# Seven block products for four in the first layer of a feed-forward block, with the second layer's split weights kept in device memory

## The chip, the cores and the metric

The kernel runs on one core of a Trainium2 chip. The metric is the device time of one execution in microseconds. The core has a matrix engine (TensorE, PE in the profile), three engines for elementwise work (VectorE or DVE, ScalarE or ACT, GpSimd or POOL), and SyncE (SP), which issues the transfers here. Each engine works through its instructions in order; semaphores order them against each other. Matmul results are accumulated in PSUM, eight banks of 128 x 512 float32; everything else lies in SBUF, 128 partitions wide.

## What is computed

An attention with keys and values pooled by eight along the sequence, then a two-layer feed-forward network with a squared ReLU. The inputs are float32 but for the two weights, which are float64.

```python
# batch 8, heads 8, sequence 576, head size 64
k_p = k.reshape(B, H, S // 8, 8, D).mean(axis=3)
v_p = v.reshape(B, H, S // 8, 8, D).mean(axis=3)
attn = softmax(q @ k_p.transpose(0, 1, 3, 2) / sqrt(D))
x = (attn @ v_p).transpose(0, 2, 1, 3).reshape(4608, 512)
h = np.maximum(x @ w_in, 0.0)          # w_in 512 x 2048
out = h * h @ w_out                    # w_out 2048 x 512
```

## The kernel before

The 4608 tokens are worked in 12 chunks of 384 (`NCH`, `CH`), the 2048 hidden columns in 16 blocks of 128 (`NFC`). One *step* is one chunk c and one block fc, so there are 192 steps. In a step TensorE does `hidden(c, fc)` (line 500), which forms h transposed, 128 hidden columns by 384 tokens, and `project(c, fc)` (line 537) of the step two before (`LAG`), which multiplies three token tiles of 128 by the 512 columns of w_out. The sums of `project` stay in three PSUM banks for a whole chunk and are stored at its end.

Chunk 0 multiplies in plain float32, which the trace lists as two matmuls for each product. From chunk 1 on every operand is split: a high half rounded to float32r (an ACT copy) and a low half, the difference (DVE); `split` on line 126 does both. A product is then three matmuls: high by high, high by low, low by high. A step of `hidden` has 4 contraction blocks x 3 = 12 matmuls of 384 columns, a step of `project` 3 tiles x 3 = 9 matmuls of 512 columns. Each matmul has a weight load of its own, 128 columns wide in these two.

The weights come as float64 words. `land` loads a tile of 512 KB, `magnitude` (two ACT operations) and `to_float32` (three DVE operations) turn it into float32, and `split_weights` (line 176) splits it; all of them share 33 slots of 4 KB a partition (`w_tile`, line 134). The 32 split tiles stay in SBUF to the end. A tile of w_in holds two blocks of 128 rows and 256 columns.

The work of a step is written out by hand from line 676: `hidden`, then TensorE's part of the attention for later chunks, then `project`, then on ACT and DVE the split of the previous step's h (`split_hidden`), what the attention stages ask for, the conversions of weights, the loads, and at the end `activate`, which takes this step's h out of PSUM (relu on ACT, the square on DVE from chunk 2 on). `at(step, f, ...)` puts a piece of other work at a step. The attention of a chunk is spread over the 22 steps before it: `STEADY` on line 86 gives for each pair of heads the step of `transpose_q`, `scores`, `exponents`, the sums' way through device memory and back, and `weigh_values` (line 470), which leaves x of that pair split in `xh` and `xl`. Two PSUM banks (`ps_h`) take turns for h.

Before step 0 the attention of chunk 0 runs alone. `FIRST` (line 82) says how many tiles of w_in are converted before it ends: their ACT part stands in the loop at line 618, and lines 585 to 588 load `FIRST + 2` weight tiles ahead of the values of batch 1 (`load_v_pair(1, p)`).

Of the kernel before, what the change touches and what calls it, by code (L numbers as in the profile page):

```python
# [37 lines left out]
def pooled_attn_relu2_ffn(  # L38
# [16 lines left out]
    PE, DVE, ACT, GP, SP = (InOrder(tc, e) for e in (nc.tensor, nc.vector, nc.scalar, nc.gpsimd, nc.sync))  # L55
# [29 lines left out]

# [6 lines left out]
    WC = 256  # L92
# [3 lines left out]
    sb = ctx.enter_context(tc.tile_pool(name="sb", bufs=2))  # L96
    dram = ctx.enter_context(tc.tile_pool(name="dram", bufs=3, space=bass.MemoryType.DRAM))
    ps_o = ctx.enter_context(tc.tile_pool(name="ps_o", bufs=1, space=bass.MemoryType.PSUM))
    ps_h = ctx.enter_context(tc.tile_pool(name="ps_h", bufs=2, space=bass.MemoryType.PSUM))
# [18 lines left out]
    def load(dst, src):  # L118
        loads.append((dst, src))
# [12 lines left out]
    raw, wf, wt = {}, {}, {}  # L132

    def w_tile(dt, name):
        return wts.tile([P, 2, 512], dt, name=name, tag="w", bufs=2 * NFC + 1)

    halves = {}

    def half_tile(kind, name):

        if kind not in halves:
            halves[kind] = w_tile(F32, name)
            return halves[kind][:, 0, :]
        return halves.pop(kind)[:, 1, :]

    def land(key):
        t = raw[key] = w_tile(U32, "raw_" + "_".join(map(str, key)))
        if key[0] == "i":
            _, cb, c0 = key
            load(t, w_in[c0 * P:(c0 + 2) * P, cb * 2 * WC:(cb + 1) * 2 * WC].rearrange("(c p) n -> p c n", p=P))  # L150
        else:
            load(t.rearrange("p a n -> p (a n)"), w_out[key[1] * P:(key[1] + 1) * P, :])

# [2 lines left out]
    def magnitude(key):  # L156

        words = raw[key].rearrange("p a (n w) -> p a n w", w=2)
        wf[key] = half_tile("f", "wf_" + "_".join(map(str, key)))
# [16 lines left out]
    def split_weights(key, eng):  # L176
        t = wt[key] = w_tile(F32R, "w_" + "_".join(map(str, key)))
        split(t[:, 0, :], t[:, 1, :], wf[key], eng)

    kv, kf, loaded = {}, {}, {}  # L180

# [271 lines left out]
    def token_turn(c, p):  # L453
# [13 lines left out]

        return then

    def weigh_values(c, p):  # L470

        if p == 0 and c == 0:
            xts[c] = sb.tile([P, NPAIR, CH], F32, name=f"x_{c}", tag="xh", bufs=2)
        elif p == 0:
            xts[c] = (sb.tile([P, NPAIR, CH], F32R, name=f"xh_{c}", tag="xh", bufs=2),
                      sb.tile([P, NPAIR, CH], F32R, name=f"xl_{c}", tag="xl", bufs=2))
        sc, rb = live.pop((c, p))
        av = ps_a.tile([P, 512], F32, name=f"av_{c}_{p}", tag="a")
        for b, o, n in segments(c):
            for i in range(2):  # L480
                PE.matmul(av[i * D:(i + 1) * D, o:o + n], lhsT=kv[b][2][:, 2 * p + i, :], rhs=sc[:, i, o:o + n],
                                 start=True, stop=True)

        def then():
            if c == 0:
                ACT.copy(xts[c][:, p, :], av[:, :CH])
                return
            xh, xl = xts[c]
            if c == 1:
                split(xh[:, p, :], xl[:, p, :], av[:, :CH])  # L490
                return
            DVE.tensor_tensor(rb, av[:, :CH], rb, op=ALU.mult)
            split(xh[:, p, :], xl[:, p, :], rb)

        return then

    gts = {}


    def hidden(c, fc):  # L500
        hp = ps_h.tile([P, 512], F32, name=f"h_{c}_{fc}", tag="h")
        cb, o = fc * P // WC, fc * P % WC
        prods = []
        for cc in range(NCC):
            key, cols = ("i", cb, cc // 2 * 2), slice(cc % 2 * WC + o, cc % 2 * WC + o + P)
            if c == 0:
                prods += [(wf[key][:, cols], xts[c][:, cc, :])]
            else:
                prods += [(wt[key][:, w, cols], xts[c][x][:, cc, :]) for w, x in ((0, 0), (0, 1), (1, 0))]
        for i, (w, x) in enumerate(prods):  # L510
            PE.matmul(hp[:, :CH], lhsT=w, rhs=x, start=i == 0, stop=i == len(prods) - 1)

        def activate():
            if c == 0:
                r = sb.tile([P, CH], F32, name=f"r_{c}_{fc}", tag="gh", bufs=LAG + 1)
            else:
                r = sb.tile([P, CH], F32, name=f"r_{c}_{fc}", tag="r", bufs=2)
            ACT.activation(r, hp[:, :CH], AF.Relu)
            if c < 2:
                ACT.activation(r, r, AF.Square)  # L520
            else:
                DVE.tensor_tensor(r, r, r, op=ALU.mult)
            gts[c, fc] = r

        return activate
# [36 lines left out]
    def at(step, f, *a):  # L562
        work.setdefault(max(step, -PRO), []).append((f, a))
# [13 lines left out]

    need = {}
    for fc in range(NFC):
        for c0 in range(0, NCC, 2):  # L580
            need.setdefault(("i", fc * P // WC, c0), fc)
        need["o", fc] = fc + LAG
    keys = sorted(need, key=need.get)
    first_keys = keys[:FIRST]
# [74 lines left out]
    for c in range(1, NCH):  # L659
        first, offsets = EARLY if c == 1 else STEADY  # L660
        names = (transpose_q, token_scores, token_normalise, token_turn, weigh_values) if c == 1 else stages
        for b, _, _ in segments(c):
            if b not in ready:
                ready.add(b)
                kv_steps(b, c * NFC + KV0)
        for p in range(NPAIR):
            s = c * NFC + first[p]
            if c > 1 or p:
                at(s - QL, load_q, c, p)
            for d, f in zip(offsets, names):  # L670
                at(s + d, f, c, p)


    last = (to_float32, split_weights)
    on_pe = (transpose_k, transpose_q, scores, token_scores, token_turn, weigh_values, pool_v_pair)
    for s in range(-PRO, len(steps) + LAG):
        todo = work.get(s, [])
        activate = hidden(*steps[s]) if 0 <= s < len(steps) else None
        later = [f(*a) for f, a in sorted(((f, a) for f, a in todo if f in on_pe), key=lambda x: x[0] is weigh_values)]
        store = project(*steps[s - LAG]) if s >= LAG else None  # L680
        if 0 <= s - 1 < len(steps):
            split_hidden(*steps[s - 1])
        for f in later:
            f()
        for f, a in todo:
            if f not in on_pe + last:
                f(*a)
        keys = [a[0] for f, a in todo if f is to_float32]
        if keys:
            to_float32(*keys)  # L690
        for f, a in todo:
            if f is split_weights:
# [35 lines left out]
```

## Time and profile before

| what | us |
|---|---|
| median of 2 runs | 971.47 (971.05 to 971.9) |
| the profiled execution | 972.07 |
| its span, first to last instruction | 970.4 |
| first matmul of `hidden` starts at | 52.59 |
| chunk 0 to the start of chunk 1 | 95.7 |
| chunk 2 to the start of chunk 3 | 76.3 |
| chunk 11 to the end of its last step's `hidden` | about 67 |

The profile page gives for each engine its busy time and the number of instructions; PEld is the weight loads, which run beside the matmuls. Matmuls overlap and their ends are modelled, so the recorded length of one (337 ns for 384 columns) is more than the time that it adds; that is read from the starts. All instructions carry line 34, the helper that issues them, and are told apart by the tiles that they write and read: `h<-xh,w_i` is a matmul that writes h from xh and a tile of w_in. A tile's name in the trace is that of the slot's kind, so `wf_o` can stand for a tile of w_in that reuses the place. The chain of waits follows the last instruction back to what released it.

### The profile page before, as it was taken

The numbers are of one execution on the slowest core, as the hardware profiler recorded it, in microseconds if no ns is written. First come the engines' busy times: TensorE is split into PE (matmuls) and PEld (weight loads), VectorE is DVE, ScalarE is ACT, GpSimd is POOL, SyncE is SP. The second block draws the span as 40 slices with busy tenths as digits, with TensorE's granted clock in tenths as the row PEclk, the third lists the DMA queues.
The fourth block names the chain that finished last, engine by engine and source line by source line (L and its number), as shares of the span: only waits on it lengthen the run. The fifth ranks groups of instructions, "written<-read, shape, count | busy, mean of one in ns | idle before, by whom it ended". The sixth has DMA issues, their size and how long they took to land.

```text
span 970.4 us, 13371 instructions
## 1 busy us (share of the span) xinstructions
PE 947.7 (98%) x4788; PEld 789.8 (81%) x4788; DVE 601.3 (62%) x1066; ACT 431.2 (44%) x911; POOL 330.7 (34%) x191
## 2 busy tenths in 40 slices
PE   7799999999999999999999999999999999999998
PEld 6455557888888888888888888888888888888997
DVE  7466778777676656667766656667677564453221
ACT  2387767675334334334434434443434433432322
POOL 4100034354344444434344344433434434440000
PEclk9589999999999999999999999999999999999999
DMA  9955002113112112112211202222311210200000
GB/s 272 336 191 158 23 7 76 43 43 101 45 45 75 32 34 73 42 41 90 60 38 48 73 17 50 66 46 54 92 41 41 76 32 18 58 9 9 33 1 32
DMA packets 105762, 63.64 MB, mean 66 GB/s; under 512 B 77840, under 2 KB 86880, under 8 KB 105696
## 3 DMA queue, kind: packets, MB, share of 16 engines
q1 hardware_dynamic: 105696, 62.79, 23.3%
q8 instruction: 37, 0.61, 0.3%
q14 instruction: 29, 0.24, 0.1%
HBM read 53.08 MB, written 9.68 MB: 65 GB/s over the span
## 4 chain that ended last, share of the span: by engine, by line
PE 89%; DMA 4%; DVE 3%; SPq 2%; ACT 1%; issue 1%; DVEq 0%; ACTq 0%
PE o L34 40%; PE h L34 40%; PE av L34 4%; PE sps L34 3%; SPq L34 2%; DMA vv<-in_v_dram 2%; DMA k<-in_k_dram 1%; PE vps L34 1%; DVE vp L34 1%; PE pps L34 1%; DMA rc<-rs 1%; DVE kp L34 0%; DVE gl L34 0%; PE kps L34 0%; DVE st L34 0%
## 5 line engine op out<-in xcount | busy, mean ns | idle before, releaser
L34 PE MATMUL h<-xh,w_i 128*128 128x384 f32 x1408 | 391.2, 338 | 0.0
L34 PE MATMUL o<-w_o,gh 128*128 128x512 f32 x1056 | 335.0, 398 | 0.0
L34 POOL PARTITION_ALL_REDUCE tot<-sc x80 | 201.5, 2566 | 223.8 <-issue 214.3
L34 PEld LDWEIGHTS h<-xh,w_i 128*128 128x128 f32 x1408 | 258.0, 188 | 8.3 <-ACT r L34 0.5
L34 PE MATMUL h<-xl,w_i 128*128 128x384 f32 x704 | 236.4, 336 | 0.0
L34 PEld LDWEIGHTS o<-w_o,gh 128*128 128x128 f32 x1056 | 192.6, 189 | 51.7 <-issue 16.5
L34 POOL PARTITION_ALL_REDUCE mx<-sc x80 | 116.5, 1504 | 301.1 <-ACT sc L34 295.0
L34 PE MATMUL o<-w_o,gl 128*128 128x512 f32 x528 | 208.8, 395 | 0.0
L34 DVE TENSOR_TENSOR r<-r 128x384 f32<-128x384 f32 x160 | 105.4, 659 | 144.6 <-ACT r L34 144.6
L34 DVE TENSOR_TENSOR gl<-r,gh 128x384 fp32r<-128x384 f32 x176 | 107.4, 610 | 79.9 <-ACT gh L34 78.3
L34 ACT ACTIVATE r<-h 128x384 f32<-128x384 f32 x192 | 94.0, 490 | 111.3 <-PE h L34 111.3
L34 ACT CAST gh<-r 128x384 fp32r<-128x384 f32 x176 | 90.4, 514 | 117.5 <-DVE r L34 116.1
L34 PEld LDWEIGHTS h<-xl,w_i 128*128 128x128 f32 x704 | 132.2, 188 | 8.2 <-issue 0.7
L34 PEld LDWEIGHTS o<-w_o,gl 128*128 128x128 f32 x528 | 99.1, 188 | 22.2
L34 DVE TENSOR_TENSOR st<-qs,st 64x384 fp32r<-64x384 f32 x80 | 70.3, 879 | 30.2 <-ACT st L34 28.9
L34 ACT CAST st<-qs 64x384 fp32r<-64x384 f32 x80 | 40.9, 511 | 47.0 <-DVE qs L34 46.0
L34 ACT ACTIVATE sc<-sc 72x384 f32<-72x384 f32 x80 | 39.7, 525 | 44.9 <-DVE sc L34 44.9
L34 ACT CAST xh<-rb 128x384 fp32r<-128x384 f32 x40 | 20.5, 513 | 81.1 <-DVE rb L34 81.1
L34 ACT COPY sc<-sps 72x384 f32<-72x384 f32 x80 | 34.1, 475 | 49.5 <-PE sps L34 49.5
L34 DVE TENSOR_REDUCE vp<-v 72x64 f32<-72x512 f32 x48 | 50.9, 1060 | 0.0
L34 PE MATMUL av<-sc,vp 72*64 72x384 f32 (+1 forms) x256 | 46.4, 448 | 2.7 <-ACT sc L34 2.7
L34 DVE TENSOR_REDUCE kp<-k 96x64 f32<-96x512 f32 x42 | 43.5, 1035 | 0.1
(93 smaller groups left out, 739.9 us busy)
## 6 DMA issues: line engine op xcount, KB each, us to landing
k<-in_k_dram SPq DMA_DIRECT2D x48, 192.0 KB
out_dram<-ob SPq DMA_DIRECT2D x36, 256.0 KB
raw_i<-in_moe_w_in_dram SPq DMA_DIRECT2D x16, 512.0 KB
raw_o<-in_moe_w_out_dram SPq DMA_DIRECT2D x16, 512.0 KB
rb<-rd SPq DMA_DIRECT2D x80, 96.0 KB
v<-in_v_dram SPq DMA_DIRECT2D x48, 144.0 KB
q<-in_q_dram SPq DMA_DIRECT2D x112, 48.0 KB
vv<-in_v_dram SPq DMA_DIRECT2D x8, 288.0 KB
```

Source lines behind the costliest of these rows:

```text
L34: return lambda *a, **k: self.tc.keep_in_program_order(f(*a, **k))
```

## The change

From chunk 2 on (`PLAIN = 2`) two steps together compute a 2 x 2 block product: two hidden blocks by two halves of the contraction on the side of the weights, two halves of the contraction by two halves of the tokens (192 each, `HT`) on the side of x. Instead of eight block products it makes seven, from sums of blocks of the weights (S1 to S4) and of x (T1 to T4). Each block product is 2 contraction blocks x 3 split terms, six matmuls of 192 columns. Four products stand in the even step, three in the odd one; between them ACT and DVE add results to each other in the PSUM banks X and Y, and later matmuls accumulate onto these sums.

- `seven` takes the place of `plain` (the old `hidden`). The two h of a pair are taken out of PSUM together at the end of the odd step, and their squares move from DVE to ACT. `split_hidden` moves from the step after to just before `project`, two steps after.
- x of a chunk is kept in float32 (`xf`), and `x_operand` forms and splits seven operands of it at the steps -9 to 0 of the chunk.
- A tile of w_in now holds 128 rows of four blocks. `split_quarter` splits its four quarters a group; `sum_of_quarters` forms and splits S1 to S4 on top. The slots are 32.
- w_out's split tiles don't stay: `store_weights` writes each to device memory at steps 10 to 25, and `fetch_weights` reads it back for each chunk from 1 on, three steps before its `project`.
- `FIRST` is 4.

```diff
+    PLAIN = 2
-    FIRST, EAGER, AHEAD = 2, 8, 5
+    FIRST, EAGER, AHEAD = 4, 8, 5
...
+    GB = 4
+    HT = CH // 2
+    SLOTS, XB, STREAM = 32, 8, 3
...
+    def split_quarter(g, e, kh):
+        split_operand(g, f"A{e}{kh}", quarter(g, e, kh))
...
+    def sum_of_quarters(g, name):
+        a, b, op = {"S1": ((1, 0), (1, 1), ALU.add), "S2": ("S1", (0, 0), ALU.subtract),
+                    "S3": ((0, 0), (1, 0), ALU.subtract), "S4": ((0, 1), "S2", ALU.subtract)}[name]
+        a, b = (sums[x] if isinstance(x, str) else quarter(g, *x) for x in (a, b))
+        t = sums[name] = in_blocks(half_tile("S", f"s_{g}_{name}"))
+        DVE.tensor_tensor(t, a, b, op=op)
+        split_operand(g, name, t)
...
+    def store_weights(fc):
+        t = w_tile(F32R, f"w_o_{fc}")
+        split(t[:, 0, :], t[:, 1, :], wf.pop(("o", fc)))
+        stored[fc] = kept.tile([P, 2, 512], F32, name=f"kept_{fc}")
+        dma(stored[fc], t.bitcast(F32))
+
+    def fetch_weights(c, fc):
+        t = wt["o", fc] = w_tile(F32R, f"w_o_{c}_{fc}")
+        load(t.bitcast(F32), stored[fc])
...
+    def x_operand(c, name):
+        one, two = xf[c][:, :2, :].rearrange("p c (h t) -> p h c t", h=2), xf[c][:, 2:, :].rearrange("p c (h t) -> p h c t", h=2)
+        if name == "T1":
+            src = temps["T"] = sb.tile([P, 2, HT], F32, name=f"t_{c}", tag="t", bufs=1)
+            DVE.tensor_tensor(src, one[:, 1], one[:, 0], op=ALU.subtract)
+        elif name == "T2":
+            src = temps["T"]
+            DVE.tensor_tensor(src, two[:, 1], src, op=ALU.subtract)
...
+        x = xts[c, name] = x_tile(F32R, f"x_{c}_{name}")
+        hi, lo = (x[:, w, :].rearrange("p (c t) -> p c t", c=2) for w in range(2))
+        split(hi, lo, src)
...
+    def seven(c, fc):
+        g, r = fc // GB, fc % GB // 2
+        if fc % 2 == 0:
+            pair["X"], pair["Y"] = (ps_h.tile([P, 512], F32, name=f"h_{c}_{fc + i}", tag="h") for i in range(2))
+        X, Y = pair["X"], pair["Y"]
+        a, b, u, d = X[:, :HT], X[:, HT:CH], Y[:, :HT], Y[:, HT:CH]
+        def product(out, wn, xn, clear=False, end=False):
+            n = 0
+            for k in range(2):
+                cols = slice((k * 2 + r) * P, (k * 2 + r + 1) * P)
+                for i, j in three:
+                    PE.matmul(out, lhsT=wt[g, wn][:, i, cols], rhs=xts[c, xn][:, j, k * HT:(k + 1) * HT],
+                              start=clear and n == 0, stop=end and n == 5, skip_group_check=True)
+                    n += 1
+        if fc % 2 == 0:
+            product(a, "A00", "B11", True)
+            product(b, "S2", "T2")
+            product(u, "S3", "T3", True)
+            product(d, "S1", "T1")
...
+            def soon():
+                ACT.copy(first, a)
+                DVE.tensor_tensor(second, b, first, op=ALU.add)
+                DVE.tensor_tensor(u, u, second, op=ALU.add)
+                DVE.tensor_tensor(b, d, second, op=ALU.add)
+            def at_end():
+                ACT.copy(third, u)
+                DVE.tensor_tensor(d, d, third, op=ALU.add)
+            return soon, at_end
+        product(b, "S4", "B22")
+        product(a, "A01", "B21", end=True)
+        product(u, "A11", "T4", end=True)
+        return [(fc - 1, X), (fc, Y)]
...
-        at(14 + int(i * 0.48), split_weights, key, DVE)
+    for i in range(NFC):
+        at(12 + i, split_quarter, i // GB, i % GB // 2, i % 2)
+        at(10 + i, store_weights, i)
+        at(4 * (5 + i // 4) + i % 4, sum_of_quarters, i // 4, f"S{i % 4 + 1}")
+        for c in range(1, NCH):
+            at(c * NFC + i + LAG - STREAM, fetch_weights, c, i)
...
+        if c >= PLAIN:
+            for d, name in ((-9, "B11"), (-2, "T1"), (-2, "T2"), (-1, "T3"), (-1, "B22"), (0, "B21"), (0, "T4")):
+                at(c * NFC + d, x_operand, c, name)
...
+        for t in (s - 2, s - 1):
+            if 0 <= t < len(steps) and (steps[t][0] < PLAIN) == (t == s - 1):
+                split_hidden(*steps[t])
         store = project(*steps[s - LAG]) if s >= LAG else None
-        if 0 <= s - 1 < len(steps):
-            split_hidden(*steps[s - 1])
+        if soon:
+            soon()
         for f in later:
             f()
...
         issue_loads()
-        for f in (activate, store):
-            if f:
-                f()
+        if activate:
+            activate()
+        for f, a in todo:
+            if f is x_operand:
+                f(*a)
+        if store:
+            store()
```

More of the change, by code (lines that the diff above doesn't have):

```diff
@@ L91, in pooled_attn_relu2_ffn @@
     NKT = H * SP_ // QT
-    WC = 256
+    GB = 4
+    HT = CH // 2
+    SLOTS, XB, STREAM = 32, 8, 3
     const = ctx.enter_context(tc.tile_pool(name="const", bufs=1))
@@ L134, in w_tile @@
     def w_tile(dt, name):
-        return wts.tile([P, 2, 512], dt, name=name, tag="w", bufs=2 * NFC + 1)
+        return wts.tile([P, 2, 512], dt, name=name, tag="w", bufs=SLOTS)
     halves = {}
@@ L148, in land @@
         if key[0] == "i":
-            _, cb, c0 = key
-            load(t, w_in[c0 * P:(c0 + 2) * P, cb * 2 * WC:(cb + 1) * 2 * WC].rearrange("(c p) n -> p c n", p=P))
+            _, g, c = key
+            load(t.rearrange("p a n -> p (a n)"), w_in[c * P:(c + 1) * P, g * 2 * GB * P:(g + 1) * 2 * GB * P])
         else:
@@ L174, in to_float32, with in_blocks, quarter, split_operand @@
             DVE.scalar_tensor_tensor(m, words[..., 1], 0x80000000, m, op0=ALU.bitwise_and, op1=ALU.bitwise_or)
-    def split_weights(key, eng):
-        t = wt[key] = w_tile(F32R, "w_" + "_".join(map(str, key)))
-        split(t[:, 0, :], t[:, 1, :], wf[key], eng)
+    def in_blocks(t):
+        return t.rearrange("p (c r n) -> p c r n", c=2, r=GB // 2)
+    def quarter(g, e, kh):
+        return wf["i", g, "both", kh].rearrange("p c (r e n) -> p e c r n", r=GB // 2, e=2)[:, e]
+    def split_operand(g, name, src):
+        t = wt[g, name] = w_tile(F32R, f"w_{g}_{name}")
+        split(in_blocks(t[:, 0, :]), in_blocks(t[:, 1, :]), src)
+    def split_quarter(g, e, kh):
+        split_operand(g, f"A{e}{kh}", quarter(g, e, kh))
+    sums = {}
+    def sum_of_quarters(g, name):
[5 more added lines that the diff above has]
+        split_operand(g, name, t)
+    stored = {}
+    def store_weights(fc):
[6 more added lines that the diff above has]
+        load(t.bitcast(F32), stored[fc])
     kv, kf, loaded = {}, {}, {}
@@ L468, in token_turn, with x_tile @@
         return then
+    def x_tile(dt, name):
+        return sb.tile([P, 2, CH], dt, name=name, tag="x", bufs=XB)
+    xf = {}
     def weigh_values(c, p):
[L472 to L476, printed above, removed]
+        if c >= PLAIN and p == 0:
+            xf[c] = sb.tile([P, NPAIR, CH], F32, name=f"xf_{c}", tag="xf", bufs=1)
         sc, rb = live.pop((c, p))
@@ L485, in then @@
             if c == 0:
[L486 to L493, printed above, removed]
-        return then
+                x = xts[c, p] = x_tile(F32, f"x_{c}_{p}")
+                ACT.copy(x[:, 0, :], av[:, :CH])
+            elif c < PLAIN:
+                x = xts[c, p] = x_tile(F32R, f"x_{c}_{p}")
+                split(x[:, 0, :], x[:, 1, :], av[:, :CH])
+            else:
+                DVE.tensor_tensor(xf[c][:, p, :], av[:, :CH], rb, op=ALU.mult)
@@ new lines, in weigh_values @@
+        return then
+    temps = {}
+    def x_operand(c, name):
[6 more added lines that the diff above has]
+            DVE.tensor_tensor(src, two[:, 1], src, op=ALU.subtract)
+        elif name == "T4":
+            src = temps["T"]
+            DVE.tensor_tensor(src, two[:, 0], src, op=ALU.subtract)
+        elif name == "T3":
+            src = one[:, 1]
+            DVE.tensor_tensor(src, two[:, 1], src, op=ALU.subtract)
+        else:
+            src = {"B11": one[:, 0], "B21": two[:, 0], "B22": two[:, 1]}[name]
+        x = xts[c, name] = x_tile(F32R, f"x_{c}_{name}")
+        hi, lo = (x[:, w, :].rearrange("p (c t) -> p c t", c=2) for w in range(2))
+        split(hi, lo, src)
@@ L497, in pooled_attn_relu2_ffn, with plain @@
     gts = {}
-    def hidden(c, fc):
+    three = ((0, 0), (0, 1), (1, 0))
+    def plain(c, fc):
         hp = ps_h.tile([P, 512], F32, name=f"h_{c}_{fc}", tag="h")
-        cb, o = fc * P // WC, fc * P % WC
+        g, o = fc // GB, fc % GB * P
+        e, r = fc % 2, fc % GB // 2
         prods = []
         for cc in range(NCC):
-            key, cols = ("i", cb, cc // 2 * 2), slice(cc % 2 * WC + o, cc % 2 * WC + o + P)
             if c == 0:
-                prods += [(wf[key][:, cols], xts[c][:, cc, :])]
+                prods += [(wf["i", g, cc][:, o:o + P], xts[c, cc][:, 0, :])]
@@ L508, in hidden @@
             else:
-                prods += [(wt[key][:, w, cols], xts[c][x][:, cc, :]) for w, x in ((0, 0), (0, 1), (1, 0))]
+                w, cols = wt[g, f"A{e}{cc // 2}"], slice((cc % 2 * 2 + r) * P, (cc % 2 * 2 + r + 1) * P)
+                prods += [(w[:, i, cols], xts[c, cc][:, j, :]) for i, j in three]
         for i, (w, x) in enumerate(prods):
             PE.matmul(hp[:, :CH], lhsT=w, rhs=x, start=i == 0, stop=i == len(prods) - 1)
-        def activate():
[L514 to L523, printed above, removed]
@@ L525, in hidden @@
-        return activate
+        return hp
+    pair = {}
+    def seven(c, fc):
[17 more added lines that the diff above has]
+            product(d, "S1", "T1")
+            first, second, third = (sb.tile([P, HT], F32, name=f"u{i}_{c}_{fc}", tag=f"u{i % 2}", bufs=1) for i in range(3))
+            def soon():
[11 more added lines that the diff above has]
+        return [(fc - 1, X), (fc, Y)]
@@ new lines, in hidden @@
+    def hidden(c, fc):
+        if c < PLAIN:
+            hps = [(fc, plain(c, fc))]
+        else:
+            hps = seven(c, fc)
+            if fc % 2 == 0:
+                return hps
+        def activate():
+            for f, hp in hps:
+                if c == 0:
+                    r = sb.tile([P, CH], F32, name=f"r_{c}_{f}", tag="gh", bufs=LAG + 1)
+                else:
+                    r = sb.tile([P, CH], F32, name=f"r_{c}_{f}", tag="r", bufs=2)
+                ACT.activation(r, hp[:, :CH], AF.Relu)
+                gts[c, f] = r
+            for f, _ in hps:
+                ACT.activation(gts[c, f], gts[c, f], AF.Square)
+        return (activate, None) if c >= PLAIN else (None, activate)
@@ L579, in pooled_attn_relu2_ffn @@
     for fc in range(NFC):
-        for c0 in range(0, NCC, 2):
-            need.setdefault(("i", fc * P // WC, c0), fc)
+        for cc in range(NCC):
+            need.setdefault(("i", fc // GB, cc), fc)
         need["o", fc] = fc + LAG
@@ L685, in pooled_attn_relu2_ffn @@
         for f, a in todo:
-            if f not in on_pe + last:
+            if f not in on_pe + last + (x_operand,):
                 f(*a)
```

15 lines of the change are left out of this document (11 added, 4 removed).

## The prediction

> **What bounds the kernel now.** I read the page first: the busy shares, the clock and the chain of waits.
>
> ```profile
> span 970.4 us, 13371 instructions
> PE 947.7 (98%) x4788; PEld 789.8 (81%) x4788; DVE 601.3 (62%) x1066; ACT 431.2 (44%) x911; POOL 330.7 (34%) x191
> PEclk9589999999999999999999999999999999999999
> PE 89%; DMA 4%; DVE 3%; SPq 2%; ACT 1%; issue 1%; DVEq 0%; ACTq 0%
> ```
>
> TensorE is the bound: 98% busy, 89% of the chain, its clock at 0.9 or more from the fourth slice on. The second number of each engine matters as much: as many weight loads (PEld) as matmuls, 4788 each. Matmuls overlap, so their recorded lengths can't be added; what they cost is the pitch, the distance from one start to the next. The chain in order of time gives that, since it takes each matmul up to the start of the next:
>
> ```profile
> 408.81 0.70 PE sps L34 x4
> 409.51 2.09 PE o L34 x9
> 411.60 2.10 PE h L34 x12
> 413.70 2.08 PE o L34 x9
> 415.79 2.11 PE h L34 x12
> ```
>
> Columns are start, length, work, count. One step is 12 matmuls h (w_in, 384 columns each, 2.10 us, pitch 175 ns) and 9 matmuls o (w_out, 512 columns, 2.08 us, 231 ns), with nothing between. The change touches h alone, in 10 chunks of 8 pairs of steps: 80 pairs at 2.10 + 2.11 = 4.21 us.
>
> **The product itself.** A pair's 24 matmuls of 384 columns become 7 products x 2 contraction blocks x 3 split terms = 42 matmuls of 192 columns. That is 8064 columns for 9216, one eighth less, but 42 weight loads of 128 columns for 24. Two prices of one matmul are possible: its 192 columns, or its weight load. For the first, the scores of an even split batch are float32r matmuls of 192 columns:
>
> ```profile
> 279.05 0.25 PE L34 MATMUL sps<-st,kl 128*72 128x192 f32 x1
> 279.14 0.25 PE L34 MATMUL sps<-st,kh 128*72 128x192 f32 x1
> ...
> 279.57 0.25 PE L34 MATMUL sps<-st,kl 128*72 128x192 f32 x1
> 279.66 0.25 PE L34 MATMUL sps<-st,kh 128*72 128x192 f32 x1
> ```
>
> Seven pitches in 0.61 us, 87 ns. There the loads have 72 columns; here they have 128. For the load (the groups of instructions by shape, the tile sps, the timeline, and the chain):
>
> ```profile
> L34 PEld LDWEIGHTS h<-xh,w_i 128*128 128x128 f32 x1408 | 258.0, 188 | 8.3 <-ACT r L34 0.5 <-issue 0.2
> L34 PEld LDWEIGHTS sps<-st,kh 128*72 128x72 f32 x104 | 14.7, 142 | 2.6 <-issue 0.4
> L34 PEld LDWEIGHTS sps<-kf,st x128: 156/162/282, 10.0 to 116.1; 64*96 64x96 f32 x128
> 78.91 0.76 PEld L34 LDWEIGHTS sps<-kf,st 64*96 64x96 f32 x16 [0.55 <-issue]
> 9.46 0.64 PE L34 MATMUL idle<-ident 128*128 128x128 f32 x4
> 76.40 2.58 PE h L34 x8
> ```
>
> A load's record is 142 ns for 72 columns, 162 (median) for 96, 188 for 128: 46 ns more for 56 columns, 0.82 ns a column, so some 105 ns of a 128-column load is streaming and the rest a fixed delay that overlaps. The fourth row shows a run that is paced by it. 16 loads of 96 columns go out as eight pairs (the two halves of the rows load side by side): (0.76 - 0.16) / 7 = 86 ns a pair. The matmuls there have only 72 columns, at chunk 0's rate (last row: 2.58 us / 8 / 384 = 0.84 ns a column) 60 ns. So 86 ns isn't the matmul; it is 96 columns of load at 0.89 ns. For 128 columns that rate gives 114 ns. The row of idle matmuls bounds it from above: loads of 128 columns under matmuls of 128, (0.64 - 0.28) / 3 = 120 ns at most.
>
> Today a load of 105 to 114 ns hides under a matmul of 175. Under 87 ns it can't, and the load becomes the pitch. I take 111 ns, in the upper half of 105 to 114 because the paced run is the nearer evidence. A pair then costs 42 x 0.111 = 4.66 us for 4.21: **0.45 us slower, 80 times: +36 us**. Bounds: 105 ns gives +16, 120 gives +66.
>
> The Trainium skill, in "TensorE: Matmul & The Clock Gate", section "LDWEIGHTS (loading the stationary operand)", has a weight load take its columns over 1.2 GHz, whatever the rows: 107 ns for 128 columns. By that figure, an estimate from the page, a pair would be 4.48 us and the 80 pairs +22 us; the trace's slope of 0.82 ns a column agrees with it, and the paced run is a little dearer.
>
> **Startup.** FIRST grows from 2 to 4, because a tile of w_in now holds 128 rows of four blocks. Two things move onto the opening chain:
>
> ```profile
> 18.47 10.54 DMA vv<-in_v_dram
> ...
> 29.14 2.80 PE vps L34 x12
> ...
> 43.87 0.66 ACT raw_i L34
> 44.53 0.54 ACT wf_i L34
> 45.07 0.57 ACT raw_i L34
> 45.64 0.74 ACT sc L34
> ...
> 52.66 2.86 PE h L34 x4
> 16.00:24.00 8.00, 4.84 (x42) 4.00 (x40) 4.96 (x13) 2.48 (x8) 7.37 (x17) 0.76 1.07 337
> 24.00:32.00 8.00, 2.86 (x14) 2.85 (x15) 3.00 (x7) 0.00 (x0) 3.25 (x8) 0.50 1.09 265
> ```
>
> The last two rows (busy time by stretch) end in the clock, the DMA share and GB/s. The loads of v for batch 1 end the first wait, at 29 us, with the DMA engines full. Six weight tiles instead of four now go ahead of them: 2 x 0.52 MB at 265 to 337 GB/s, 3.1 to 4.0 us. Then the ACT work on two more tiles (two operations each, 0.57 to 0.66 us) is put before the copy sc that the chain waits for: 4 x 0.65 = 2.6 us. From 52.66 on the chain is TensorE without a gap, so nothing gives it back: **+6 us** (0 to 7; 0 if other transfers were what filled the DMA engines).
>
> **The other engines in the steady state.**
>
> ```profile
> L34 ACT ACTIVATE r<-h 128x384 f32<-128x384 f32 x192 | 94.0, 490 | 111.3 <-PE h L34 111.3
> L34 ACT ACTIVATE r<-r 128x384 f32<-128x384 f32 x32 | 16.8, 524 | 1.0
> L34 ACT CAST kh<-kps 128x288 fp32r<-128x288 f32 x12 | 4.8, 398 | 20.8 <-PE kps L34 20.8
> L34 DVE TENSOR_TENSOR r<-r 128x384 f32<-128x384 f32 x160 | 105.4, 659 | 144.6 <-ACT r L34 144.6
> L34 DVE TENSOR_TENSOR rb<-av,rb 128x384 f32<-128x384 f32 x40 | 22.2, 554 | 3.9 <-PE av L34 3.9
> L34 DVE TENSOR_TENSOR xl<-rb,xh 128x384 fp32r<-128x384 f32 x40 | 22.4, 559 | 23.2 <-ACT xh L34 23.2
> 120.00:200.00 80.00, 80.00 (x343) 57.43 (x342) 63.69 (x110) 55.20 (x113) 33.56 (x16) 1.00 0.15 40
> 440.00:520.00 80.00, 78.59 (x398) 67.03 (x397) 57.70 (x96) 31.52 (x68) 32.39 (x17) 1.00 0.23 60
> ```
>
> Per pair ACT gains two squares (0.52 each) and two copies of 192 columns (from 490 ns at 384 and 398 at 288, about 0.31): 1.7 us on a pair of some 9. At 31.5 of 80 us busy it has room. DVE loses two squares of 0.66 and gains four sums of 192 columns (half of 554 ns and a fixed part, about 0.36): no change. So neither becomes the bound by load; what matters is the order. The first pair of sums has to be in PSUM before the odd step's first product; TensorE does project's 2.08 us in between, and two sums take 0.8. X is free for the next pair once its relu (0.49) is done; that also has project's 2.08 us. If ACT or DVE lags by over a microsecond that cover is gone and TensorE waits for all of the lag.
>
> Such a place is the chunk border. Seven operands of x in place of four, four of them with a sum first: 4 x 0.55 + 7 x 0.56 = 6.1 us of DVE for 2.2, all but one operand within steps -2 to 0, behind which the low halves of h wait in DVE's order. TensorE asks for T4 in step 1, 3.4 us after step 0's four products (project 2.08, two products 1.33). DVE and ACT get there after the pair's sums (1.5), B21's cast and low half (1.1), T4's sum (0.55), cast and low half (1.1), with hand-overs 4.4: 1.0 late. The same count gives 0.4 for the low half of h behind T1 and T2 at step -1, and 0.3 for T3. These are estimates from the rows above: 1.7 us a chunk, **+17 us** for ten (0 to 40, the upper end being half a microsecond in every pair).
>
> In chunk 1 and early 2 the splits go from 32 to 48 (16 quarters, 16 sums, 16 of w_out), and 16 sums come with them. DVE is at 63.7 of 80 us there. Steps 20 to 25 hold a quarter, a store and a sum each, about 1.4 us more of DVE a step than now, against 16.3 / 80 of a 4.7 us step, 0.95, of room: six steps fall 2.7 us behind. I take **+4 us** (0 to 10), since weights, sums and fetched tiles also share 32 slots there.
>
> **The transfers.** Sixteen stores and 11 x 16 fetches of 512 KB add 101 MB, some 119 GB/s over steps of 4.4 us; the chip moved 337 GB/s above, so a fetch takes 1.6 us and has three steps, 13 us. On SP it waits for the slot of the tile used four steps before; behind it stand the next step's small transfers, which are not due before that step. Cost 0; without that cover it would be 1.6 us a step.
>
> **The sum.** 970.4 + 36 + 6 + 17 + 4 = 1033.4 of span, and the 1.7 us by which this execution's time, 972.07, is above its span: 1035 us. That execution is 0.6 us above the median of 971.47.
>
> **The rivals.** *A, the columns are the price.* If a load hides under 87 ns, a pair costs 42 x 0.087 = 3.65 us, 0.56 less: -45 us, and with the same +27 elsewhere 954 us; without the 17 and 4, 933. For it: no row shows a load of 128 columns as the only limit. Against: the paced run. It decides at 42 x p = 4.21 - 27/80, a pitch of 92 ns. I give it 0.16, faster by over 2% in 0.07 of that. The skill's section "Back-to-back issue gap" on the same page has a rule that leads here: columns over 2.4 GHz plus 2.5 ns, 82.5 ns for 192, an estimate of 3.47 us a pair; the trace has 87 for that shape and 175 instead of 162.5 for 384.
>
> *B, a partly hidden load.* At 100 ns a pair is 4.20, no change, and the rest makes it 970.4 + 27 + 1.7 = 999. Chance 0.10, half of it within 2%.
>
> *C, the pair's chain isn't covered.* The loads as forecast, and ACT or DVE behind in most pairs by half a microsecond: 1035 + 40 = 1075 and up. For it: DVE's sums stand in order behind the transposes and reductions of later chunks. Against: 2 us of cover. 0.08.
>
> **How the numbers follow.** The forecast has 0.66, with its own range of 1000 (105 ns, +16, a few us of startup and borders) to 1070 (115 ns or full borders). The range of all, 975 to 1085, leaves out most of A and the end of C. Over 2% (19 us, about what a measurement can tell): slower 0.66 + 0.08 + 0.05 = 0.79; same 0.05 + 0.09 = 0.14; faster 0.07.
>
> **What would show it.** The pitch of the new h matmuls of 192 columns: 105 to 114 ns if I am right, 87 if A is. PEld's busy share should rise while TensorE's columns fall. The first h at about 59 us instead of 52.6. Gaps on TensorE at every sixteenth step, few elsewhere. The forecast fails if loads overlap more than the paced run shows, or if the waits in a pair are long.

## The result, and the profile after

The changed kernel takes 1102.53 us (median of 2 runs, 1101.64 to 1103.42) where the kernel before took 971.47: a ratio of 1.135, 95% interval 1.130 to 1.140. It is slower, as forecast, but by 131 us where 64 were forecast, and outside the range, which ended at 1085.

The page of the changed kernel, the lines that answer to those of before (span, busy shares, clock, shares of the chain of waits):

```profile
span 1099.9 us, 17495 instructions
PE 1018.3 (93%) x6228; PEld 837.4 (76%) x6228; DVE 697.2 (63%) x1328; ACT 545.0 (50%) x1277; POOL 334.2 (30%) x191
PEclk9589999996999999999999999999999999999999
PE 47%; DVE 25%; ACT 14%; DMA 9%; issue 3%; SPq 2%; DVEq 0%; ACTq 0%
```

TensorE has gone from 89% of the chain to 47%, and DVE and ACT together hold 39%, while their busy shares are only 63% and 50%. That is the mark of waits, not of a new engine at its limit. The chain in order of time shows the new shape of a pair where nothing is waited for:

```profile
533.01 1.99 PE h L34 x18
535.00 0.70 PE sps L34 x4
535.69 2.10 PE o L34 x9
537.79 2.67 PE h L34 x24
```

24 matmuls of 192 columns in 2.67 us and 18 in 1.99: 111 ns each, and 4.66 us a pair, the forecast figure to the digit. So the product costs what was predicted, and the missing time lies elsewhere. The starts of the first h of each chunk tell where. The table gives chunk lengths in us, for chunks 3 to 10 the mean; "idle" is TensorE's time beyond a pitch of 111 ns (192 columns), 174 ns (384) or 231 ns (512) between matmuls of h and o, gaps over 60 ns alone, per chunk of chunks 3 to 10, at the steps 2, 6, 10, 14 and at the steps 15, 0, 1 of a chunk. The other rows are the experiments below.

| kernel | time | first h | chunk 1 | chunk 2 | 3 to 10 | 11 and end | idle 2, 6, 10, 14 | idle 15, 0, 1 |
|---|---|---|---|---|---|---|---|---|
| before | 971.5 | 52.6 | 75.7 | 76.3 | 74.3 | 75.2 | 0.4 | 0 |
| changed | 1102.5 | 57.3 | 91.1 | 101.7 | 84.4 | 79.9 | 3.9 | 2.4 |
| late | 1081.7 | 56.5 | 90.9 | 100.2 | 82.1 | 79.9 | 0.4 | 2.6 |
| notot | 1051.9 | 56.7 | 83.0 | 97.5 | 79.8 | 79.6 | 0.4 | 1.9 |
| oldx | 1078.2 | 54.9 | 91.4 | 100.7 | 81.9 | 79.3 | 4.2 | 0.1 |
| alias | 1081.3 | 57.2 | 80.1 | 88.8 | 84.8 | 79.9 | 4.2 | 2.4 |
| rest | 1023.5 | 56.1 | 80.9 | 84.7 | 78.2 | 79.2 | 0.4 | 0.1 |
| bare | 1016.6 | 56.0 | 81.4 | 81.9 | 77.7 | 79.2 | 0.4 | 0 |

The span grew by 129.5 us: 4.7 up to the first h, -0.8 in chunk 0, 15.4 in chunk 1, 25.4 in chunk 2, 10.0 in each of chunks 3 to 10, and 4.7 in chunk 11 to the end. Of the 10.0 the weight loads are 3.6 (8 pairs at 0.45), the steps 2, 6, 10, 14 are 3.5 and the border 2.4. The last column leaves out a gap that follows the small matmuls of the scores: at step 15 TensorE then waits another 0.6 us a chunk in the changed kernel, 1.4 in late, and nothing in before, oldx, rest and bare.

A difference of 2 or 3 us between two totals says little here: the kernel before, timed again beside the experiments, took 968.5 to 973.7 us, and the first h comes at 54.9 to 57.3 us in the changed kernel and its variants, although their opening is the same.

What the waits look like, in the chain at step 6 of chunk 5:

```profile
545.38 1.31 ACT r L34 x3
546.69 0.82 ACT sc L34 x2
547.51 0.41 ACT st L34
547.95 1.39 DVE st L34
549.37 0.55 DVE st L34
549.95 1.93 DVE gl L34
551.92 1.89 PE o L34 x7
```

Read it backwards. TensorE's o waits for the low half of h (gl). On DVE that stands behind the two low halves of a transposed q (st), these wait for ACT's casts, and on ACT the casts stand behind exponentials of the scores (sc) and the relu and the squares (r) of the step before. One st takes 1.39 us beside another of 0.55, and gl takes 1.93, three times its usual 0.6. The timeline has a possible reason beside it:

```profile
547.26 5.04 POOL L34 PARTITION_ALL_REDUCE tot<-sc  x2 [7.63 <-issue]
547.42 1.03 ACT L34 CAST st<-qs 64x384 fp32r<-64x384 f32 x2
547.95 1.97 DVE L34 TENSOR_TENSOR st<-qs,st 64x384 fp32r<-64x384 f32 x2 [1.70 <-ACT st L34]
549.95 1.91 DVE L34 TENSOR_TENSOR gl<-r,gh 128x384 fp32r<-128x384 f32 x1
```

GpSimd's two all-reduces tot run from 547.26 to 552.30, over all three. The st of 0.55 us lies under them as well, so not every operation there is slow: of the low halves st and gl of the whole trace that overlap a tot, 61 of 107 took over 0.8 us, and none of the 112 that overlap no all-reduce. Whether the all-reduce is the cause, the run notot tells.

### The profile page after: what moved, and what is told of

It is laid out like the page before. It is cut to its first block, busy times and chain, and to the rows that moved or that the text cites. A ratio compares the mean times of both kernels' runs of the same rounds, so it can differ in the third digit from the quotient of the medians.

```text
span 1099.9 us, 17495 instructions
## 1 busy us (share of the span) xinstructions
PE 1018.3 (93%) x6228; PEld 837.4 (76%) x6228; DVE 697.2 (63%) x1328; ACT 545.0 (50%) x1277; POOL 334.2 (30%) x191
## 4 chain that ended last, share of the span: by engine, by line
PE 47%; DVE 25%; ACT 14%; DMA 9%; issue 3%; SPq 2%; DVEq 0%; ACTq 0%
PE h L34 23%; PE o L34 20%; DVE gl L34 6%; DVE st L34 6%; ACT r L34 4%; ACT sc L34 3%; PE sps L34 2%; DVE h L34 2%; DMA rb<-rd 2%; DVE x_T L34 2%; ACT st L34 2%; SPq L34 2%; ACT x_T L34 2%; DMA vv<-in_v_dram 2%; DVE kp L34 2%
## 5 line engine op out<-in xcount | busy, mean ns | idle before, releaser
L34 PE MATMUL h<-x_T,w_S 128*128 128x192 f32 x1440 | 177.4, 276 | 9.1 <-ACT x_T L34 8.0
L34 PEld LDWEIGHTS h<-x_T,w_S 128*128 128x128 f32 x1440 | 169.4, 193 | 10.6 <-ACT x_T L34 8.7
L34 PEld LDWEIGHTS o<-w_o,gl 128*128 128x128 f32 x528 | 100.2, 190 | 61.5 <-DVE gl L34 39.9
L34 PE MATMUL h<-x_B,w_A 128*128 128x192 f32 x960 | 134.2, 274 | 6.1 <-DVE x_B L34 5.0
L34 PEld LDWEIGHTS h<-x_B,w_A 128*128 128x128 f32 x960 | 127.1, 192 | 15.2 <-DVE x_B L34 6.4
L34 DVE TENSOR_TENSOR h<-h,u 128x192 f32<-128x192 f32 x240 | 87.4, 364 | 36.8 <-PE h L34 25.4
L34 ACT ACTIVATE r<-r 128x384 f32<-128x384 f32 x192 | 91.0, 517 | 1.0
L34 PE MATMUL h<-x_T,w_A 128*128 128x192 f32 x480 | 71.2, 280 | 7.2 <-DVE h L34 3.3
L34 PEld LDWEIGHTS h<-x_B,w_S 128*128 128x128 f32 x480 | 65.9, 191 | 7.0
L34 PEld LDWEIGHTS h<-x_T,w_A 128*128 128x128 f32 x480 | 61.3, 193 | 11.6 <-DVE h L34 4.5
L34 PE MATMUL h<-x_B,w_S 128*128 128x192 f32 x480 | 64.8, 270 | 0.0
```

Source lines behind the costliest of these rows:

```text
L34: return lambda *a, **k: self.tc.keep_in_program_order(f(*a, **k))
```

## The experiments

### Is the weight load the floor of a matmul's pitch?

The kernel before, with h's 384 columns cut in two in five chunks (`x` and the output sliced alike).

```diff
+    WIDTHS = {3: (192, 192), 5: (256, 128), 7: (224, 160), 9: (288, 96), 10: (320, 64)}
...
-        for i, (w, x) in enumerate(prods):
-            PE.matmul(hp[:, :CH], lhsT=w, rhs=x, start=i == 0, stop=i == len(prods) - 1)
+        cuts = WIDTHS.get(c, (CH,))
+        o = 0
+        for k, n in enumerate(cuts):
+            for i, (w, x) in enumerate(prods):
+                PE.matmul(hp[:, o:o + n], lhsT=w, rhs=x[:, o:o + n], start=k == 0 and i == 0,
+                          stop=k == len(cuts) - 1 and i == len(prods) - 1, skip_group_check=True)
+            o += n
```

> The kernel before, with the 384 columns of h cut in two in five chunks: chunk 3 into 192 + 192, 5 into 256 + 128, 7 into 224 + 160, 9 into 288 + 96, 10 into 320 + 64. Columns as before, weight loads doubled. If the weight load is the floor of a matmul's pitch: 111 ns for every piece up to 224 columns, 117 for 256, 131 for 288, 146 for 320; a step's h grows from 2.10 us to 2.66 (chunks 3 and 7), 2.74 (5), 2.90 (9), 3.08 (10), in all some 57 us more, 1028 us. If columns are the price: 87 ns for 192, 58 for 128, 30 for 64, and 972 us.

Measured: 1023.75 us. The 24 matmuls of a step in the chain, from chunks 3, 5, 9 and 10 in this order:

```profile
303.27 2.65 PE h L34 x24
...
486.76 2.73 PE h L34 x24
...
799.19 2.85 PE h L34 x24
...
864.25 3.02 PE h L34 x24
```

From the starts, the median pitches are 111 to 112 ns for 64, 96, 128, 160, 192 and 224 columns alike, 120 for 256, 131 for 288, 147 for 320, 174 for 384. A floor of 111 ns holds up to 224 columns; above it the columns are the price. That the floor is the load's, and not a fixed price of any matmul, is seen from the scores: matmuls of 192 columns too, but with loads of 72 columns, start 89 ns apart (median, same run). Other widths of load were not tried. Rivals A and B fall.

### Is it the order, or GpSimd?

The run late moves transpose_q, from chunk 2 on, behind the PSUM sums of its step:

```diff
-        later = [f(*a) for f, a in sorted(((f, a) for f, a in todo if f in on_pe), ...
+        later = [f(*a) for f, a in sorted(((f, a) for f, a in todo if f in on_pe and not (f is transpose_q and a[0] > 1)), ...
...
         for f in later:
             f()
+        for f, a in todo:
+            if f is transpose_q and a[0] > 1:
+                f(*a)()
```

> The changed kernel, with transpose_q from chunk 2 on moved behind the PSUM sums and the low half of h in its step. Theory 1 (order: the transposes' ACT and DVE work, which itself waits for the relus of the step before, stands ahead of the low half that project waits for): the idle time of TensorE at steps 2, 6, 10, 14, now 3.9 us a chunk, falls under 1, chunks 3 to 10 get 2.5 to 3.5 us shorter, in all 1072 to 1082 us. Theory 2 (GpSimd: the low half takes 1.9 instead of 0.6 us while an all-reduce runs, wherever it stands): at most a third of it goes, 1092 to 1100 us. Theory 3 (the lateness only moves, to the scores of the next step): 1095 to 1105 us with waits at steps 3, 7, 11, 15.

Measured: 1081.7 us, 20.8 less, in the range of theory 1. The idle time at steps 2, 6, 10, 14 is back at that of the kernel before. Some of it has only moved, as theory 3 has it: at step 15 TensorE waits 0.8 to 0.9 us a chunk longer (the lines stand under "What is left"). But the run doesn't clear GpSimd: its low halves still reach 1.90 us, only earlier, where nobody waits. So the all-reduce was taken away instead, with the order left as it was. This kernel sends the maxima where the sums of the exponents would go.

```diff
-        tots = reduced("tot", c, p)
+        tots = mx
...
-            GP.partition_all_reduce(tots[i], sc[:, i], channels=SP_, reduce_op=bass_isa.ReduceOp.add)
```

> The changed kernel without GpSimd's second all-reduce (tot, the sum of the exponents); the maxima are sent in its place. Theory 1 (the order of the transposes alone makes the low half late): TensorE's idle time at steps 2, 6, 10, 14 stays over 2.5 us a chunk of 3.9. Theory 2 (it needs both, the order and the slow DVE operations that coincide with tot, 1.4 for st and 1.9 for the low half instead of 0.55 and 0.6): it falls under 0.8, 1070 to 1080 us. The border's 2.4 us a chunk stays by both.

Measured: 1051.9 us. The idle time at those steps is gone as well (0.4 us a chunk), the border keeps 1.9. The groups of instructions by shape, st and gl, of the changed kernel and then of this one:

```profile
L34 DVE TENSOR_TENSOR gl<-r,gh 128x384 fp32r<-128x384 f32 x176 | 137.3, 780 | 96.5 <-ACT gh L34 93.5
L34 DVE TENSOR_TENSOR st<-qs,st 64x384 fp32r<-64x384 f32 x80 | 76.8, 960 | 81.6 <-ACT st L34 80.4
```
```profile
L34 DVE TENSOR_TENSOR gl<-r,gh 128x384 fp32r<-128x384 f32 x176 | 102.1, 581 | 103.8 <-ACT gh L34 101.3
L34 DVE TENSOR_TENSOR st<-qs,st 64x384 fp32r<-64x384 f32 x80 | 44.2, 553 | 82.8 <-ACT st L34 81.6
```

The mean (the number after the busy time) of gl falls from 780 to 581 ns, of st from 960 to 553. Theory 2 holds: the wait needs both, the order and the slow operations; take either away and it is gone from these steps. The time fell much further than the 1070 to 1080 expected, by 50.6 us, the most of any single edit: chunk 1 by 8.1, chunk 2 by 4.2, and chunks 3 to 10 by 4.6 each, of which 3.5 at the steps 2, 6, 10, 14 and most of the rest at the border, which was expected to stay. With the slow operations the run also takes GpSimd's own 2.5 us for each sum out of the attention's path; no run separates the two.

The Trainium skill, in "SBUF — State Buffer", section "Who interferes with whom", says that a VectorE instruction with two inputs in SBUF contends with a GpSimd instruction that reads SBUF. st and gl are such instructions, and the trace agrees in part: 1.4 to 1.9 us for many of them under tot, 0.55 and 0.58 on average without it, but 46 of the 107 that overlap a tot took no more than 0.8 us.

### The chunk border

The run oldx forms no operands of x after chunk 2; later chunks multiply by those of chunk 2.

```diff
-            for d, name in ((-9, "B11"), ...
+            for d, name in () if c > PLAIN else ((-9, "B11"), ...
...
-rhs=xts[c, xn][:, j, k * HT:(k + 1) * HT]
+rhs=xts[PLAIN, xn][:, j, k * HT:(k + 1) * HT]
```

> The changed kernel without forming the seven operands of x from chunk 3 on; the products use those of chunk 2. Theory 1 (the operands formed at steps -2 to 0 hold up DVE and ACT at the chunk border): TensorE's idle time at steps 15, 0 and 1, now 2.4 us a chunk, falls under 0.5, that at steps 2, 6, 10, 14 stays near 3.9, chunks 3 to 10 get 1.5 to 2.5 us shorter, 1080 to 1090 us. Theory 2 (reductions and transposes do it, not the operands): less than 0.7 us a chunk, over 1095 us.

Measured: 1078.2 us, 24.4 less, and the idle time at the border falls from 2.4 to 0.1 us a chunk: theory 1, a little more than expected. Of the 24.4 us, 2.4 come from the start (first h at 54.9 instead of 57.3), which the operands can't cause; some 22 are theirs. In the changed kernel's chain at step 1 one sees the lateness that the forecast had put there:

```profile
520.74 0.27 DVE h L34
521.01 0.46 DVE x_B L34
521.47 0.48 DVE t L34
521.97 0.52 ACT x_T L34
522.52 0.57 DVE x_T L34
523.09 0.04 issue
523.13 0.82 PE h L34 x5
```

After the last PSUM sum (h) come B21's low half, T4's sum, cast and low half, 2.1 us, and then TensorE's matmul with T4.

The run lateend has late's edit and moves the last PSUM sum of an even step (`at_end`) ahead of the step's other work on DVE:

```diff
+        if soon and activate:
+            activate()
         for f, a in todo:
             if f is transpose_q and a[0] > 1:
...
-        if activate:
+        if activate and not soon:
             activate()
```

> The changed kernel with transpose_q behind the PSUM sums, as in the run late, and besides the last sum of an even step (d) moved ahead of the step's reductions and other work. Theory 1 (TensorE waits for d because it stands behind reductions of k and v, 1 us each, on DVE): the waits before h with A11 and T4 at steps 5, 9, 11, some 0.5 us a chunk, go and those at step 1 shrink, 4 to 9 us less than late's 1081.7, 1073 to 1078 us. Theory 2 (the sum isn't late, T4 is): within 2 us of late.

Measured: 1082.8 us against late's 1081.7. The waits at steps 5, 9 and 11 went as expected, but steps 15, 0 and 1 rose from 2.6 to 3.3 us a chunk: no gain. At the border it is the operands that are late.

### Chunks 1 and 2

The run alias forms no sums of weights; quarters stand in their place.

```diff
-        t = sums[name] = in_blocks(half_tile("S", f"s_{g}_{name}"))
-        DVE.tensor_tensor(t, a, b, op=op)
-        split_operand(g, name, t)
+        wt[g, name] = wt[g, {"S1": "A00", "S2": "A01", "S3": "A11", "S4": "A00"}[name]]
```

> The changed kernel without the 16 sums S1 to S4 of weights and their splits; the products take quarters in their place. Theory 1 (sums and splits crowd DVE and ACT in steps 20 to 35): chunk 2 falls from 101.7 us to 84 to 90, what the later chunks take, and chunk 1 by some us, in all 1075 to 1087 us. Theory 2 (the first fetches and the slots hold chunk 2): chunk 2 stays over 95 us. Chunks 3 to 11 unchanged by either.

Measured: 1081.3 us; chunk 1 falls by 11.0 and chunk 2 by 12.9, to 88.8. Theory 1. Busy time by stretch over the first 17 us of chunk 2, which starts at 243.3 us in the changed kernel and at 232.2 in this one (PE, PEld, DVE, ACT, POOL, clock, DMA share and GB/s):

```profile
243.00:260.00 17.00, 9.54 (x40) 7.69 (x39) 12.42 (x24) 6.40 (x15) 2.87 (x2) 0.70 0.32 80
```
```profile
232.00:249.00 17.00, 15.39 (x92) 12.82 (x90) 11.04 (x23) 8.72 (x20) 6.56 (x4) 0.90 0.51 179
```

TensorE is busy for 9.5 of 17 us in the one and 15.4 in the other. But DVE is at 12.4 of 17 and ACT at 6.4, so neither is full. The changed kernel's waits name what goes on instead, the first two rows over the whole run, the third from 243 to 260 us (us in total, times, longest):

```profile
ACT w_S L34 <- DVE s_S L34: 27.8, 10, 6.1
DVE w_S L34 <- ACT w_S L34: 13.0, 16, 2.6
```
```profile
PE h L34 <- ACT x_T L34: 7.0, 2, 4.8
```

ACT stands up to 6.1 us for DVE's sum before it can cast it, with the casts of the x operands, relus and high halves of h behind it in order, and DVE then waits for the cast. TensorE waits 7.0 us for two of those casts of x operands. That this handing to and fro is the cost, rather than the work, is read from the waits; no run separates the two.

The clock column shows a further cost. After TensorE had stood idle, its granted clock was 0.5 from 248.3 to 258.6 us and from 262.0 to 268.8. Matmuls of 192 columns then start 214 ns apart instead of 111, those of 512 columns 427 instead of 233. TensorE was busy for 12.6 us of these stretches, so an estimate of the loss is half of that, some 6 of the 25.4 us by which chunk 2 grew. In the kernel before, no such stretch lies between 58 us and its last 2 us; in alias chunk 2 has two of 3.4 us. What brings the clock down was not tested.

The transfers were tried by themselves: the run stream is the kernel before with w_out stored and fetched as in the change.

```diff
-        at(14 + int(i * 0.48), split_weights, key, DVE)
+        if key[0] == "i":
+            at(14 + int(i * 0.48), split_weights, key, DVE)
+    for i in range(NFC):
+        at(10 + i, store_weights, i)
+        for c in range(1, NCH):
+            at(c * NFC + i + LAG - 3, fetch_weights, c, i)
```

> The kernel before, with the changed kernel's way of w_out alone: stored at steps 10 to 25, fetched for every chunk, nothing else. Theory 1 (the stores stand in order on SP and hold up the attention's small transfers behind them until DVE has split the tile): chunk 1 grows by 5 to 12 us from 75.8, the chunks from 3 on stay at 74 to 76, 977 to 984 us. Theory 2 (only the added splits and sums of w_in crowd DVE): chunk 1 within 2 us of 75.8, 971 to 974 us. If the fetches cost something in the steady state: chunks 3 to 10 over 77 us each.

Measured: 977.4 us, chunk 1 at 83.8 (+8.1), chunks 3 to 10 at 74.1 (74.3 before). In the steady state the fetches, 92 MB in all, cost nothing. To tell the SP queue from the transfers themselves, strdefer issues each store two steps after its split, at the step's end:

```diff
-        dma(stored[fc], t.bitcast(F32))
+        halfway[fc] = t
...
+    def send_weights(fc):
+        load(stored[fc], halfway.pop(fc).bitcast(F32))
...
+        at(12 + i, send_weights, i)
```

> The run stream (the kernel before with w_out stored and fetched) with each store issued two steps after its split and behind the step's small transfers. Theory 1 (SP stands waiting for DVE's split): chunk 1, 83.8 us in stream and 75.7 before, falls to 75.5 to 79. Theory 2 (the DMA engines, at some 0.75 of their time in chunk 1 for 0.2 before, land the attention's small transfers late): it stays at 82 to 85 us.

Measured: 971.9 us, where the kernel before took 968.5 beside it; chunk 1 is at 76.5. SP's waits from 100 to 260 us, in stream and then in strdefer:

```profile
SPq L34 <- DVE w_o L34: 67.0, 13, 32.7
```
```profile
SPq L34 <- DVE w_o L34: 18.0, 1, 18.0
```

Theory 1: a store put on SP at once holds the queue until DVE has split the tile, and the attention's small transfers stand behind it. Of 13 such waits one is left, and all but 0.8 of the 8.1 us are back, at no lower load on the DMA engines (a share of 0.71 to 0.83 from 152 to 243 us, 0.67 to 0.79 in stream).

In the changed kernel the same edit (run defer) did little:

> The changed kernel, with each store of a w_out tile issued on SP two steps after its split and at the step's end, behind the small transfers, where the low half is long done. Theory 1 (in chunk 1 SP stands waiting for DVE's split, and the attention's transfers behind it come late): chunk 1 falls from 91.1 us to 81 to 86, chunk 2 hardly changes, 1092 to 1098 us. Theory 2 (the splits and sums on DVE and ACT set chunk 1 whatever the queue): 89 to 92 us, 1100 to 1103 us.

Measured: 1101.1 us; chunk 1 falls by 3.4 to 87.7, between the two theories, and the total by no more than 1.4. In the changed kernel the sums of weights are the larger cost there: 11.0 us of chunk 1 in alias.

Moving the stores to ACT's queue (run qact) did harm:

```diff
-        dma(stored[fc], t.bitcast(F32))
+        ACT.dma_start(stored[fc], t.bitcast(F32))
```

> The changed kernel, with the 16 stores of w_out's tiles issued from ACT's queue instead of SP's. Theory 1 (stores hold SP's queue in chunk 1): chunk 1 falls from 91.1 us to 78 to 84, chunk 2 hardly changes, 1090 to 1096 us. Theory 2 (DVE's splits and sums set chunk 1): chunk 1 stays at 89 to 92 us, 1100 to 1103 us.

Measured: 1119.9 us, which neither theory foresaw; chunk 1 is at 100.3. Here ACT does the waiting for DVE's split (25.6 us in 12 waits, "ACT r <- DVE w_o" in its waits), with the relus behind it. Another 7 us are in chunks 3 to 10, which take 85.3 us each; five stretches of 3.4 us at a granted clock of 0.5 lie there, none in the changed kernel.

### What is left

The run rest puts the edits of late, oldx and alias together.

> The edits of late, alias and oldx together: transposes behind the sums, no sums of weights, no operands of x formed after chunk 2. If the three costs are separate, they add: 1102.5 - 20.8 - 21.2 - 24.4 = 1036 us, and what is left over 971 is the weight loads (about 36), the start (about 5), the transfers and quarters in chunk 1 (about 8) and little else, idle time of TensorE in chunks 3 to 10 under 1 us each. If they hide behind each other: 1045 us or more.

Measured: 1023.5 us, 79 less than the changed kernel where the three edits alone give 66. They more than add, and the traces show two reasons. The first is that late moves some lateness to step 15. There TensorE, behind the scores, waits for ACT's cast of h (gh), in the changed kernel and then in late:

```profile
PE o L34 <- ACT gh L34: 4.0, 8, 0.5
```
```profile
PE o L34 <- ACT gh L34: 11.4, 8, 1.4
```

That is one wait in each of chunks 3 to 10, 7.4 us more in late; rest has none of them. Two causes meet there, and removing one leaves the other. The second is the clock: in chunks 3 to 10 late has one stretch of 3.4 us at a granted clock of 0.5, oldx two and alias two, the changed kernel and rest none. By an estimate from late's chunk 8 (86.7 us with such a stretch, 85.1 for chunk 5 without) each costs some 1.6 us, 8 in all.

The run bare is rest without the sums between the products in PSUM:

```diff
-            return soon, at_end
+            return None, None
```

> The run rest without the sums in PSUM between the products (no ACT copies, no DVE additions). If the pair's chain is covered by project, as forecast: within 3 us of rest. If TensorE waits for it in most pairs (rival C): 10 to 40 us less than rest.

Measured: 1016.6 us, 7 less than rest, between the two expectations. The sums themselves cost little, as forecast, but not nothing: 2.8 us in chunk 2, and 0.6 in each of chunks 3 to 10, where TensorE waits for them at the steps 1, 5, 9 and 11. In bare a pair is matmul after matmul:

```profile
509.22 2.66 PE h L34 x24
511.87 2.10 PE o L34 x9
513.97 1.99 PE h L34 x18
```

Chunks 3 to 10 take 77.7 us for 74.3: the weight loads alone, 3.4 us a chunk. With halves of 192 columns, and a load of 128 columns for every matmul, a pair costs 0.45 us more whatever the other engines do: even bare, with all that is left out of it, is 45 us slower than the kernel before. Halves of 256 columns, where the floor hardly bites, were not tried; they need chunks of 512 tokens and another division of PSUM.

## Why the prediction was right in direction and wrong in size

The forecast had 63 us more of span, 129.5 came. By stretch: start and chunk 0 are +3.9 for +6 forecast; chunks 1 and 2 are +40.8 for some 9 (the 4, and chunk 2's tenth of the 36 and of the 17); chunks 3 to 10 are +80 for 42; chunk 11 is +4.7 for 5. So two steps of the forecast failed: the cover in the steady state (with the border, 38 us too little) and the work in chunks 1 and 2 (some 31 us too little).

- **What bounds the kernel, and the price of a product: right.** 111 ns was taken between 105 and 114, and 111 was measured, in the changed kernel and, by itself, in widths. That the choice between 105 and 114 met it to the digit is luck; the floor is not. 42 x 0.111 = 4.66 us a pair; +36 us forecast, 3.4 a chunk in bare. Rivals A and B had 0.26 of the chances and were wrong. The sign that PEld's busy share would rise did not come: it fell from 81% to 76%, since the span grew by more than its busy time (789.8 to 837.4 us).
- **Startup: right.** +6 forecast, +4.7 measured, +3.5 as the mean over all runs with the new opening against those with the old. The loads of v end at 31.4 instead of 29.0 us, and ACT's work on four tiles takes 4.5 us instead of 2.2 on the chain.
- **The transfers at 0: right for the steady state** (stream, 74.1 us a chunk), **wrong in chunk 1.** The forecast looked at what the fetch waits for on SP, and not at the store, which waits for DVE at the head of the same queue: 8.1 us in stream, 3.4 in the changed kernel (defer).
- **The chunk border, +17: right mechanism, under-sized.** 1.7 us a chunk were added up from the queues (0.4 at step 15, 0.3 at step 0, 1.0 at step 1); 3.0 were measured (0.9, 0.4 and 1.7, with the wait behind the scores), and some 22 us came off without the operands.
- **"What matters is the order", with no cost outside the border: a step that failed.** The forecast set 2 us of cover against chains of 0.8 us. It took 0.6 us for a low half and, away from the border, put nothing ahead of it. In fact transpose_q's transpose and two low halves stand ahead of it on DVE in every fourth step, their casts stand on ACT behind relus, squares and exponentials, and two of the DVE operations run at 1.4 and 1.9 us under the all-reduce. So the gaps came at every fourth step, and not at every sixteenth alone: 3.9 us of idle time a chunk for 0.4, 20.8 us in late, and 50.6 in notot, where the border and chunks 1 and 2 gain too. The page of before showed the slow operations:

```profile
L34 DVE TENSOR_TENSOR st<-qs,st 64x384 fp32r<-64x384 f32 x80 | 70.3, 879 | 30.2 <-ACT st L34 28.9
```

The mean of 879 ns is well over the 553 of notot and the 554 to 559 of the other operations with two inputs in the forecast's rows. In the kernel before the low half had a whole step of slack; with split_hidden just ahead of project it has none.

- Part of the same step was a misreading: the odd step's relus and squares come back from `hidden` in the first place of the pair, as `soon`, and so stand right behind `project`, not at the end of the step as the text ahead of the result has it. They are earlier than assumed, and in the chain at step 6 they stand, with the exponentials, ahead of the casts of st.
- **Chunks 1 and 2, +4 of other work: the term that was mis-sized most.** 40.8 us more, some 31 beyond all that was forecast there. The forecast compared busy times (1.4 us more of DVE a step against 0.95 of room). The sums of weights with their splits cost 23.9 us there with DVE not full; the waits put this down to ACT and DVE waiting for each other, and TensorE for the operands of x behind them; the stores cost 3.4; and the granted clock of 0.5 in chunk 2, some 6 us, of which alias has some 3 less, is a term that the forecast did not have.
- **Rival C** came true in its total, and half of it in its reason: ACT and DVE behind in order, but at every fourth step, the border and chunks 1 and 2, not in most pairs; the PSUM sums are covered nearly everywhere (7 us in bare).

## What to carry to other kernels

Fewer columns is less time only above the floor that the weight load sets: find that floor in the trace (a run of short matmuls with wide loads) before counting multiplications. Look at the granted clock of a stretch before reading its busy times. When a consumer is moved next to its producer's neighbour in program order, list what stands ahead of it on each in-order engine in every phase of the schedule, and take the slow cases of each operation, not the means. An operation that waits, put at the head of a shared queue, costs what stands behind it; in the kernel before, the same store two steps later was nearly free.

## What the runs showed of the hardware

- A matmul with a weight load of 128 columns has a pitch of 111 ns from 64 to 224 columns of float32r, in one kernel at one granted clock (widths, clock 1.0 in those chunks); at 256 it is 120, a little above what the slope from 288 (131) to 384 (174) would give. With a load of 72 columns, 192 columns have a pitch of 89 ns in the same run.
- VectorE operations on two SBUF inputs (st and gl) took up to 1.9 instead of about 0.55 us while GpSimd's second all-reduce ran: 61 of 107 over 0.8 us in the changed kernel. While the first one ran, 8 of 37 low halves of h were over 0.8 us there; in the kernel before 28 of 44 took 0.73 to 0.83.
- At a granted clock of 0.5, matmuls of 192 columns started 214 ns apart and those of 512 columns 427, for 111 and 233 at 1.0 (changed kernel, chunk 2).
- 92 MB of fetches beside the kernel's own 63 MB, in transfers of 512 KB, left every chunk from 3 on as it was (stream, 74.1 us for 74.3).
